# Clustered attention and SwiGLU on one core: routing sims on 16 PE tiles, head group 1 turned by PE, V sums on PE, and a new order on SP and Pool

## The chip, the core and the metric

The kernel runs on one core of one Trainium2 chip. Its engines are named as the profile names them: PE (TensorE, matrix products), PEld (its weight loads), DVE (VectorE), ACT (ScalarE), POOL (GpSimd) and SP, whose queue issues nearly all DMAs. A name with a q, as SPq, is the sequencer of that engine. The metric is the time of one execution in microseconds (us). An execution is counted as slow, and kept out of the ratios, when it is over 1.5% above the fastest of its kernel. One execution of the kernel before, of 369.8 us, is (1.8% above 363.1). A profile is of one execution, and its span is about 1.8 us shorter than the time of the same execution.

## The reference, cut to what matters

```python
# B, H, S, D = 4, 8, 768, 64; 16 clusters; d_model 512, d_ff 1536
q_assign = argmax(q_n @ c_n.T)          # "sims": nearest centroid of each query
k_assign = argmax(k_n @ c_n.T)          # and of each key
mask     = q_assign[:, None] == k_assign[None, :]
attn     = softmax(where(mask, q @ k.T / sqrt(D), -1e9))
x        = (attn @ v)                   # laid out as [B*S, H*D]
out      = (silu(x @ w_gate) * (x @ w_val)) @ w_out
```

## The kernel before

The order on each engine is the order in which the program emits its operations. The emission is driven by *units*. A unit is two score matmuls, one exponential and six value matmuls; there are 192 (4 batches, 2 halves of the queries, 8 heads, 3 pairs of key blocks). From unit 31 on, FFN matmuls are put between those of the attention. Heads come in 8 groups of four; groups 0 and 1 are batch 0. `put(u, f, ...)` emits `f` after unit `u`.

The sims: 32-row, 32-column products in fp32, each in its own tile of the PE array, first for two of the four row groups (8 tiles), then for the other two. Each half uses one of the two score slots (tag `sc`), except for group 1.

```python
def route_sims(qi, bp):                       # bp = 0, 1: half of the rows
    ...
    for t in range(2):
        for s in range(2):
            for bb in range(2):
                p0 = 32 * (2 * bp + bb)
                for i in range(4):
                    nc.tensor.matmul(
                        out=sps[bb][32 * i:32 * i + 32, 0:SH // 2],
                        lhsT=c4[p0:p0 + 32, 4 * g + i, s, t, :],
                        rhs=qts[(qi, i)][p0:p0 + 32, t, :, s, :], ...)
    ...
    nc.vector.transpose(out=dst, in_=sp[:, :, 0:SH // 2])
```

Only group 0 is turned to [D, tokens] by PE; all others by DMA transposes, each of which waits at the head of the SP queue for Pool's cast:

```python
if qi == 0:   # 12 PE transposes into PSUM, two ScalarE copies
    ...
else:
    nc.sync.dma_start_transpose(out=qka..., in_=nb...)
```

The V sums of groups 2 to 7 are a VectorE reduction and one fp32 matmul with ones. The attention output `xn` of a head pair becomes a column block of `xall` by a DMA transpose, emitted at once. Weights are loaded in 18 pieces into 4 staging buffers and cast by Pool.

The softmax here doesn't subtract the row's maximum and nothing guards it: scores larger than these inputs give would overflow.

## Time and profile before

The median is 365.0 us (363.1 to 369.8). Unit 0 starts at 18.2 us, the first FFN matmul is at 52.8. The table of windows of the kernel before (for each stretch: length, then busy us and count of PE, PEld, DVE, ACT, POOL, then the granted PE clock, DMA share, GB/s; the DMA share is the summed time of the packets over that of 16 DMA engines, and can exceed 1):

```profile
18.00:30.00 12.00, 10.66 (x212) 6.80 (x212) 9.79 (x19) 6.51 (x9) 0.96 (x2) 1.00 1.06 161
30.00:42.00 12.00, 9.84 (x87) 6.01 (x86) 8.71 (x13) 6.97 (x10) 6.01 (x6) 0.72 1.12 301
42.00:52.00 10.00, 8.71 (x107) 4.19 (x103) 3.45 (x6) 9.21 (x13) 6.80 (x7) 1.00 1.10 347
52.00:66.00 14.00, 9.75 (x86) 5.76 (x85) 6.64 (x12) 8.07 (x13) 5.39 (x6) 1.00 1.10 320
66.00:90.00 24.00, 21.63 (x293) 13.70 (x293) 20.06 (x35) 12.34 (x19) 12.44 (x18) 1.00 1.03 227
90.00:120.00 30.00, 26.23 (x308) 15.55 (x312) 18.86 (x31) 14.62 (x23) 5.32 (x8) 0.94 0.72 180
120.00:320.00 200.00, 198.56 (x2173) 123.36 (x2183) 126.37 (x228) 134.68 (x201) 34.59 (x49) 1.00 0.42 100
```

From 120 us on PE is hardly idle (busy 198.56 of 200 us), so there only PE work counts. Before that it is, and the DMA engines are full from 18 to 90 us. Between 30 and 42 us the clock was at one half for part of the time (33.6 to 40.5 in the clock records). What PE waited for, longest first (us in total, times, longest):

```profile
PE vp L395 <- DVE ug L415: 4.2, 3, 1.7
PE sc L336 <- DMA qka<-ohT: 2.6, 2, 2.3
PE gp L395 <- DMA xall<-xn: 2.0, 1, 2.0
PE sc L336 <- DVE qka L214: 1.9, 2, 1.6
PE acc L362 <- ACT pt_118 L343: 1.3, 5, 0.4
PE gp L395 <- DVE hT L425: 1.3, 1, 1.3
```

From the timeline of the same kernel (start, length, engine, line, operation, out<-in, then the idle time before it and what ended it). The SP queue spends 18.1 to 26.6 us on four DMA transposes of group 1. Only then comes the first weight load, and Pool, which casts it, sat idle for 10 us. ScalarE lost 3.75 us to the sims of group 1:

```profile
18.14 1.36 SPq L244 DMA_TRANSPOSE qka<-nb_93  x1
...
24.60 1.98 SPq L244 DMA_TRANSPOSE qka<-nb_96  x1
...
26.62 1.40 SPq L202 DMA_DIRECT2D wt<-in_moe_w_gate_dram  x1
...
27.90 0.81 ACT L343 ACTIVATE pt_120<-sc 128x768 bf16<-128x768 f32 x1 [3.75 <-PE sc L336]
...
32.43 1.17 POOL L206 CAST wg_sb<-wt 128x1024 bf16<-128x1024 f32 x1 [10.15 <-DMA wt<-in_moe_w_gate_dram]
```

The sims of a later group, in the stretch where PE is full. Each half takes 1.46 us from its first start to the next matmul:

```profile
163.76 1.53 PE L269 MATMUL sp<-qt,c_68 32*32 32x192 f32 x64
...
165.22 0.50 PE L336 MATMUL sc<-qka 80*128 80x384 bf16 x2
...
167.14 1.53 PE L269 MATMUL sp<-qt,c_68 32*32 32x192 f32 x64
...
168.60 0.50 PE L336 MATMUL sc<-qka 80*128 80x384 bf16 x2
```

### The profile page before, as it was taken

What the parts mean: (1) busy time and instruction counts of PE and PEld (TensorE: products, weight loads), DVE (VectorE), ACT (ScalarE), POOL (GpSimd) and SP (SyncE); (2) the same over time, 40 slices, a digit from 0 to 9 for tenths busy, and PEclk for the clock granted to TensorE, in tenths of its full rate; (3) what the DMA queues carried; (4) which work ended last, traced back from release to release, by engine and by line L of the source; (5) the groups of instructions that cost most, each with busy time, mean ns of one, the idle gap of its engine ahead of it and who ended that gap; (6) DMA issues with size and microseconds to landing.
All of it is one profiled execution on the core that took longest, in us unless ns stands there. A gap on an engine that the chain in (4) does not pass through costs nothing.

```text
span 363.9 us, 9129 instructions
## 1 busy us (share of the span) xinstructions
PE 341.2 (94%) x3751; PEld 210.6 (58%) x3770; DVE 226.6 (62%) x403; ACT 220.0 (60%) x328; POOL 82.9 (23%) x118
## 2 busy tenths in 40 slices
PE   8987978896898899999999999999999999999995
PEld 6854535563465565666556665666566656665652
DVE  7779425779249966586828784777636614660770
ACT  5546785454356546674667656765677777774431
POOL 5513564715203300141003300420100100000000
PEclk9998799999899999999999999999999999999999
DMA  7699999999687532895267513962220011002102
GB/s 239 244 189 268 287 278 365 259 186 263 132 252 174 84 73 58 265 211 56 60 201 205 112 24 84 324 140 34 61 70 11 14 42 68 13 13 70 40 0 86
DMA packets 82712, 50.55 MB, mean 139 GB/s; under 512 B 59248, under 2 KB 77680, under 8 KB 82672
## 3 DMA queue, kind: packets, MB, share of 16 engines
q1 hardware_dynamic: 82528, 49.95, 54.6%
q8 instruction: 29, 0.48, 0.6%
q14 instruction: 11, 0.09, 0.1%
q10 hardware_dynamic: 144, 0.03, 0.0%
HBM read 28.34 MB, written 6.29 MB: 95 GB/s over the span
## 4 chain that ended last, share of the span: by engine, by line
PE 68%; DMA 14%; DVE 6%; SPq 6%; POOL 3%; issue 2%; ACT 1%; DVEq 0%; POOLq 0%; ACTq 0%
PE o_ps L437 16%; PE gp L395 13%; PE vp L395 13%; PE sc L336 12%; PE acc L362 7%; DMA wt<-in_moe_w_gate_dram 5%; PE sp L269 4%; SPq L244 4%; DMA qk<-in_k_dram 4%; PE gv L395 2%; DMA vs<-in_v_dram 2%; DMA qka<-ohT 2%; DMA wt<-in_moe_w_out_dram 2%; DVE qt L223 2%; DVE ug L415 1%
## 5 line engine op out<-in xcount | busy, mean ns | idle before, releaser
L336 PE MATMUL sc<-qka 80*128 80x384 bf16 x384 | 96.1, 332 | 4.5 <-DMA qka<-ohT 2.6
L415 DVE SCALAR_TENSOR_TENSOR ug<-th,gp 128x384 f32<-128x384 f32 x90 | 49.2, 547 | 52.2 <-ACT th L413 51.9
L395 PE MATMUL vp<-xall,wv_sb 128*128 128x384 bf16 x360 | 73.2, 325 | 4.5 <-DVE ug L415 4.2
L395 PE MATMUL gp<-xall,wg_sb 128*128 128x384 bf16 x360 | 73.4, 325 | 3.2 <-DMA xall<-xn 2.0
L381 POOL TENSOR_TENSOR xn<-num,rec 128x384 bf16<-128x384 f32 x28 | 23.1, 826 | 211.2 <-DVE rec L379 143.2
L437 PE MATMUL o_ps<-wo_sb,hT 128*128 128x512 bf16 x269 | 70.1, 384 | 1.0
L343 ACT ACTIVATE pt_118<-sc 128x768 bf16<-128x768 f32 x48 | 39.0, 812 | 38.7 <-PE sc L336 38.1
L425 DVE TENSOR_TENSOR hT<-ug,vp 128x384 bf16<-128x384 f32 x90 | 49.4, 549 | 10.2 <-PE vp L395 3.2
L413 ACT ACTIVATE th<-gp 128x384 f32<-128x384 f32 x90 | 43.9, 488 | 18.7 <-PE gp L395 15.8
L395 PEld LDWEIGHTS <-wv_sb 128*128 128x128 bf16 x384 | 37.2, 97 | 30.8 <-issue 5.9
L395 PEld LDWEIGHTS <-wg_sb 128*128 128x128 bf16 x384 | 37.2, 97 | 29.5 <-issue 3.9
L343 ACT ACTIVATE pt_121<-sc 128x768 bf16<-128x768 f32 x48 | 38.9, 811 | 20.6 <-PE sc L336 20.6
L343 ACT ACTIVATE pt_119<-sc 128x768 bf16<-128x768 f32 x48 | 38.9, 811 | 17.9 <-PE sc L336 17.5
L343 ACT ACTIVATE pt_120<-sc 128x768 bf16<-128x768 f32 x48 | 39.0, 812 | 17.7 <-PE sc L336 15.8
L437 PEld LDWEIGHTS <-hT 128*128 128x128 bf16 x288 | 28.1, 98 | 29.4 <-issue 2.0
L223 DVE STREAM_TRANSPOSE qt<-qk 128x768 f32<-128x768 f32 x32 | 30.7, 963 | 7.4 <-DMA qk<-in_k_dram 7.3
L336 PEld LDWEIGHTS <-qka 80*128 80x128 bf16 x384 | 25.4, 99 | 10.2 <-issue 6.3
L269 PE MATMUL sp<-qt,c_68 32*32 32x192 f32 x1024 | 24.6, 324 | 0.2 <-DVE sT L280 0.2
L442 ACT ACTIVATE o_sb<-o_ps 128x512 f32<-128x512 f32 x24 | 14.4, 598 | 12.1 <-PE o_ps L437 12.1
L362 PEld LDWEIGHTS <-pt_118 128*128 128x128 bf16 x288 | 14.8, 98 | 11.7 <-ACT pt_118 L343 4.2
L362 PEld LDWEIGHTS <-pt_120 128*128 128x128 bf16 x288 | 15.0, 98 | 11.1 <-ACT pt_120 L343 3.2
L374 DVE TENSOR_TENSOR num<-acc,vsb_109 128x390 f32<-128x390 f32 x12 | 6.7, 561 | 22.0 <-PE acc L362 22.0
(115 smaller groups left out, 349.7 us busy)
## 6 DMA issues: line engine op xcount, KB each, us to landing
vs<-in_v_dram SPq DMA_DIRECT2D x16, 384.0 KB, 5.4
out_dram<-o_sb SPq DMA_DIRECT2D x24, 256.0 KB, 2.2
qk<-in_q_dram SPq DMA_DIRECT2D x14, 384.0 KB, 5.2
qk<-in_k_dram SPq DMA_DIRECT2D x14, 384.0 KB, 5.7
wt<-in_moe_w_gate_dram SPq DMA_DIRECT2D x6, 512.0 KB, 6.0
wt<-in_moe_w_val_dram SPq DMA_DIRECT2D x6, 512.0 KB, 6.1
wt<-in_moe_w_out_dram SPq DMA_DIRECT2D x6, 512.0 KB, 7.3
qka<-ohT SPq DMA_DIRECT2D x24, 48.0 KB, 2.1
```

Of the source, the lines that this page charges most:

```text
L223: nc.vector.transpose(out=qt.rearrange("p t j s i -> p (t j s i)"), in_=qk.rearrange("p t j d -> p (t j d)"))
L244: nc.sync.dma_start_transpose(out=qka.rearrange("p t j n -> p (t j) n"), in_=nb.rearrange("p t j c -> p (t j c)"))
L269: nc.tensor.matmul(out=sps[bb][32 * i:32 * i + 32, 0:SH // 2], lhsT=c4[p0:p0 + 32, 4 * g + i, s, t, :], rhs=qts[(qi, i)][p0:p0 + 32, t, :, ...
L336: nc.tensor.matmul(out=sc[:, jj, 0:SH], lhsT=qka[0:KA, 1, j, :], rhs=qka[0:KA, 0, JH * hf:JH * hf + JH, :], start=True, stop=True)
L343: nc.scalar.activation(out=pt, in_=sc[:, :, 0:SH], func=ACT.Exp, scale=SCALE)
L362: nc.tensor.matmul(out=acc[:, h % 2, a, :], lhsT=pt[:, jj, ts(a, 128)], rhs=va[:, h % 4, j, :], start=(h % 2 == 0 and j == 0 and a == 0), ...
L381: (nc.vector if xc == 0 and qi < NQ else nc.gpsimd).tensor_tensor(out=xn.rearrange("p a h d -> p h a d"), in0=num[:, :, :, 0:D], in1=rec.t ...
L395: nc.tensor.matmul(out=ps, lhsT=w[:, c, ts(fb, 128)], rhs=xall[:, ch % XR, c, :], start=(c == 0), stop=(c == DMC - 1))
L413: nc.scalar.activation(out=th, in_=gp, func=ACT.Tanh, scale=0.5)
L415: nc.vector.scalar_tensor_tensor(out=ug, in0=th, scalar=1.0, in1=gp, op0=ALU.add, op1=ALU.mult)
L425: nc.vector.tensor_tensor(out=hTs[ch][:, fb, :], in0=ug, in1=vp, op=ALU.mult)
L437: nc.tensor.matmul(out=ops[0], lhsT=hT[:, fc, ts(ob, 128)], rhs=wo_sb[:, fc, :], start=(fc == 0), stop=(fc == DFC - 1))
```

## The change

The intent: run the sims of a group in one burst on all 16 tiles, holding both score slots at once, with FFN matmuls issued before the next scores; turn group 1 by PE and ScalarE like group 0, so that the SP queue and the DMA engines are free for weights; move V sums from VectorE to PE; and reorder loads. Weight casts were on Pool already; what moves to Pool are group 0's V casts. The diff, cut to its core:

```diff
-    W1 = 40                 # warming matmuls (they only keep PE busy) before unit 0
+    W1 = 8                  # now put twice, so 16
+    XD = 4                  # units by which three of the first four x transposes are put off
     def sum_v(qi):                            # groups 2 to 7, as group 0 and 1 before
-        nc.vector.tensor_reduce(out=vs1, in_=vaugs[qi % NV]..., op=ALU.add)
-        ... one fp32 matmul with ones_f
+        for j in range(J):
+            nc.tensor.matmul(out=vp, lhsT=ones_b, rhs=vaugs[qi % NV][:, :, j, :], ...)
     def cast_v(qi, i):
-        copy(nc.scalar if qi == 0 else nc.gpsimd, ...)
+        copy(nc.gpsimd, ...)
     def prep_cast(qi, i):
-        if qi == 0:
+        if qi < NQ:                           # group 1 too: PE transposes, ScalarE copies
     def route_sims(qi, rows=4, tag="sc", part=0):
-                for bb in range(2):
-                    p0 = 32 * (2 * bp + bb)
+                    for bb in range(rows):
+                        p0 = 32 * (b0 + bb)
     def normalise(...):
+        if xc or qi >= NQ:
+            turn_x(xc, m)
+        else:
+            put(cur[0] + (XD if m < 3 else 0), turn_x, xc, m)
-    wu = [3, 5, 6, 8, 9, ..., 31]; the last five loads (14th to 18th) not before unit 26
+    wu = [2, 3, 5, 6, 8, 9, ..., 30]; each load one unit after the cast that frees its buffer
-            w0 = (30, 42)[n] if b == 1 else ...
+            w0 = (28, 42)[n] if b == 1 else ...
-            for bp in range(2):
-                put(w0 + 8 + bp, route_sims, qi, bp)
+            put(w0 + 8, route_sims, qi)
+            early.add(w0 + 9)                 # scores of this unit after its FFN matmuls
-            warm(W2)
+            warm(3 if ui < 8 else W2)
... (group 1's sims in two units; its mask copies in units 7, 14 and 15, not all in 6;
...  group 0's V sum one unit earlier; `xn` of batch 0's second half on VectorE, not Pool)
```

More of the change, by code (lines that the diff above doesn't have):

```diff
@@ L120 @@
            for i in range(NV)]
-    ones_f = persist.tile([128, 128], FP32, name="ones_f")
-    nc.gpsimd.memset(ones_f, 1.0)
     ones_b = persist.tile([128, 128], BF16, name="ones_b")
@@ L140, in cast_v, with sum_v @@
     def cast_v(qi, i):
-        copy(nc.scalar if qi == 0 else nc.gpsimd,
-             vaugs[qi % NV][:, i, :, 0:D], vst.pop((qi, i)))
-    def sum_v0(qi):
+        copy(nc.gpsimd, vaugs[qi % NV][:, i, :, 0:D], vst.pop((qi, i)))
+    def sum_v(qi):
         vp = psum.tile([128, 4, D + 1], FP32, name="vsq", tag="f", bufs=3)
         for j in range(J):
-            nc.tensor.matmul(out=vp, lhsT=ones_b, rhs=vaugs[qi][:, :, j, :],
+            nc.tensor.matmul(out=vp, lhsT=ones_b,
+                             rhs=vaugs[qi % NV][:, :, j, :],
                              start=(j == 0), stop=(j == J - 1))
-        nc.vector.tensor_scalar_mul(vsb[qi], vp, TINY)
-    vs1s = {}
-    def sum_v(qi):
-        vs1 = sb.tile([128, 4, D + 1], FP32, name="vs1", tag="num", bufs=2)
-        nc.vector.tensor_reduce(
-            out=vs1, in_=vaugs[qi % NV].rearrange("p i j c -> p i c j"),
-            axis=AX.X, op=ALU.add)
-        vs1s[qi] = vs1
-    def sum_vm(qi):
-        vs1 = vs1s.pop(qi)
-        vp = psum.tile([128, 4 * (D + 1)], FP32, name="vsp", tag="f", bufs=3)
-        nc.tensor.matmul(out=vp, lhsT=ones_f,
-                         rhs=vs1.rearrange("p i c -> p (i c)"),
-                         start=True, stop=True)
-        nc.vector.tensor_scalar_mul(
-            vsb[qi % NV].rearrange("p i c -> p (i c)"), vp, TINY)
+        nc.vector.tensor_scalar_mul(vsb[qi % NV], vp, TINY)
     NP = 4
@@ L221, in prep_turn @@
         qk = qk_tiles[(b, 4 * g + i)]
-        qt = sb.tile([128, 2, J, 2, 32], FP32, name="qt", tag="qt", bufs=4)
+        spare = qi == 1 and i == 0
+        qt = sb.tile([128, 2, J, 2, 32], FP32, name="qt",
+                     tag="hT" if spare else "qt", bufs=1 if spare else 4)
         nc.vector.transpose(out=qt.rearrange("p t j s i -> p (t j s i)"),
@@ L251, with route_sims @@
     rmaxs = {}
-    def route_sims(qi, bp):
+    def route_sims(qi, rows=4, tag="sc", part=0):
         b, g = quads[qi]
-        if bp == 0:
+        if part == 0:
             routes[qi] = sb.tile([128, 2, 2 * J, 2, NCL], FP32, name="sT",
                                  tag="sT", bufs=2)
-        if qi == 1:
-            sps = [psum.tile([128, 512], FP32, name="sp", tag="f", bufs=3)
-                   for _ in range(2)]
-        else:
-            sp = psum.tile([128, 2, 512], FP32, name="sp", tag="sc", bufs=2)
-            sps = [sp[:, bb] for bb in range(2)]
-        for t in range(2):
-            for s in range(2):
-                for bb in range(2):
-                    p0 = 32 * (2 * bp + bb)
-                    for i in range(4):
-                        nc.tensor.matmul(
-                            out=sps[bb][32 * i:32 * i + 32, 0:SH // 2],
-                            lhsT=c4[p0:p0 + 32, 4 * g + i, s, t, :],
-                            rhs=qts[(qi, i)][p0:p0 + 32, t, :, s, :],
-                            start=(t == 0 and s == 0),
-                            stop=(t == 1 and s == 1),
-                            skip_group_check=True)
-        dst = routes[qi][:, bp].rearrange("p m t c -> p (m t c)").rearrange(
-            "p (b n) -> p b n", b=2)
-        if qi == 1:
-            for bb in range(2):
-                nc.vector.transpose(out=dst[:, bb],
-                                    in_=sps[bb][:, 0:SH // 2])
-        else:
-            nc.vector.transpose(out=dst, in_=sp[:, :, 0:SH // 2])
@@ new lines, in route_sims @@
+        for b0 in (rows * part,):
+            if tag == "sc":
+                sps = [psum.tile([128, 2, 512], FP32, name="sp", tag="sc",
+                                 bufs=2) for _ in range(rows // 2)]
+                ps = [sps[bb // 2][:, bb % 2] for bb in range(rows)]
+            else:
+                sps = [psum.tile([128, 1, 512], FP32, name="sp", tag="f",
+                                 bufs=3) for _ in range(rows)]
+                ps = [sps[bb][:, 0] for bb in range(rows)]
+            for t in range(2):
+                for s in range(2):
+                    for bb in range(rows):
+                        p0 = 32 * (b0 + bb)
+                        for i in range(4):
+                            nc.tensor.matmul(
+                                out=ps[bb][32 * i:32 * i + 32, 0:SH // 2],
+                                lhsT=c4[p0:p0 + 32, 4 * g + i, s, t, :],
+                                rhs=qts[(qi, i)][p0:p0 + 32, t, :, s, :],
+                                start=(t == 0 and s == 0),
+                                stop=(t == 1 and s == 1),
+                                skip_group_check=True)
+            n = rows // len(sps)
+            for m, sp in enumerate(sps):
+                c0 = (b0 + n * m) * J
+                nc.vector.transpose(
+                    out=routes[qi].rearrange("p a m t c -> p (a m) t c")[
+                        :, c0:c0 + n * J].rearrange(
+                            "p m t c -> p (m t c)").rearrange(
+                                "p (b n) -> p b n", b=n),
+                    in_=sp[:, :, 0:SH // 2])
@@ L380, in normalise, with turn_x @@
         xn = sb.tile([128, JH, 2, D], BF16, name="xn", tag="xn", bufs=2)
-        (nc.vector if xc == 0 and qi < NQ else nc.gpsimd).tensor_tensor(
+        (nc.vector if qi < NQ else nc.gpsimd).tensor_tensor(
             out=xn.rearrange("p a h d -> p h a d"), in0=num[:, :, :, 0:D],
             in1=rec.to_broadcast([128, 2, JH, D]), op=ALU.mult)
+        xns[(xc, m)] = xn
+        if xc or qi >= NQ:
+            turn_x(xc, m)
+        else:
+            put(cur[0] + (XD if m < 3 else 0), turn_x, xc, m)
+    xns = {}
+    cur = [0]
+    def turn_x(xc, m):
         nc.sync.dma_start_transpose(
             out=xall[:, xc, m, :].rearrange("p (a t) -> p a t", a=JH),
-            in_=xn.rearrange("p a h d -> p (a h d)"))
+            in_=xns.pop((xc, m)).rearrange("p a h d -> p (a h d)"))
     hTs = {}
@@ L501 @@
     centroids_T(1)
-    for i in range(2, 4):
-        prep_turn(0, i)
+    prep_turn(0, 2)
     prep_cast(0, 2)
+    prep_turn(0, 3)
+    prep_turn(1, 0)
+    route_sims(0)
+    prep_cast(0, 3)
     for bp in range(2):
-        route_sims(0, bp)
         route_max(0, bp)
-    prep_cast(0, 3)
     route_hot(0)
@@ L511 @@
         route_back(0, t)
-    warm(W1)
+    for i in range(2):
+        prep_cast(1, i)
+        warm(W1)
     for i in range(4):
@@ L515 @@
     load_v(1, 1)
-    for i in range(4):
-        prep_cast(1, i)
     for i in range(2):
@@ L523 @@
     put(0, load_w, 3)
-    put(0, prep_turn, 1, 0)
-    put(0, prep_turn, 1, 1)
-    put(0, prep_mask, 0, 2, nc.vector)
-    put(0, prep_turn, 1, 2)
-    put(0, prep_turn, 1, 3)
-    put(0, prep_mask, 0, 3, nc.vector)
-    put(3, sum_v0, 0)
+    for i in range(1, 4):
+        put(0, prep_turn, 1, i)
+    for i in range(2, 4):
+        put(0, prep_mask, 0, i, nc.vector)
+        put(i, prep_cast, 1, i)
+        put(1, cast_v, 1, i - 2)
+        put(1, cast_v, 1, i)
+    put(2, sum_v, 0)
     for bp in range(2):
-        put(S1, route_sims, 1, bp)
-        put(S1, route_max, 1, bp)
-    put(S1, route_hot, 1)
+        put(S1 + bp, route_sims, 1, 2, "f", bp)
+        put(S1 + bp, route_max, 1, bp)
+    put(S1 + 1, route_hot, 1)
     for t in range(2):
-        put(S1, route_back, 1, t)
+        put(S1 + 1, route_back, 1, t)
     for i in range(4):
-        put(S1 + 1, prep_mask, 1, i, nc.vector)
-        put(1, cast_v, 1, i)
-    put(13, sum_v0, 1)
-    wu = [3, 5, 6, 8, 9, 10, 12, 13, 15, 16, 18, 19, 26, 27, 28, 29, 30, 31]
+        put(S1 + 2 + (0, 0, 7, 8)[i], prep_mask, 1, i, nc.vector)
+    put(13, sum_v, 1)
+    wu = [2, 3, 5, 6, 8, 9, 10, 12, 13, 15, 16, 18, 19, 26, 27, 28, 29, 30]
     for i in range(len(wjobs)):
@@ L544 @@
         if i + 4 < len(wjobs):
-            put(wu[i] + 1 if i < 9 else max(wu[i] + 1, 26), load_w, i + 4)
+            put(wu[i] + 1, load_w, i + 4)
+    early = set()
     for b in range(1, B):
@@ L549 @@
             qi = NQ * b + n
-            w0 = (30, 42)[n] if b == 1 else u0 + (P0, P1)[n]
+            w0 = (28, 42)[n] if b == 1 else u0 + (P0, P1)[n]
             for m in range(2):
@@ L558 @@
                 put(w0 + 14 + i, prep_mask, qi, i, nc.sync)
-            put(w0 + 15, sum_v, qi)
-            put(w0 + 19, sum_vm, qi)
+            put(w0 + 16, sum_v, qi)
+            put(w0 + 8, route_sims, qi)
+            early.add(w0 + 9)
             for bp in range(2):
-                put(w0 + 8 + bp, route_sims, qi, bp)
                 put(w0 + 9 + bp, route_max, qi, bp)
@@ L570 @@
     for ui, u in enumerate(units):
-        pt = att_scores(u)
+        cur[0] = ui
+        if ui not in early:
+            pt = att_scores(u)
         if ui < 24:
-            warm(W2)
+            warm(3 if ui < 8 else W2)
         want = per * min(
@@ L581 @@
             fpos += 1
+        if ui in early:
+            pt = att_scores(u)
         if pend is not None:
```

## The prediction

> **What bounds the kernel now.** Three stages, by the table of windows.
> 1. 18 to 52.7 us, attention alone (units 0 to 30; unit 31 brings the first FFN matmul, at 52.7). An exponential takes 0.81 us, so 31 units need 25 us; they take 34.5. Lost: ScalarE idles 3.7 us behind the sims of head group 1 (timeline), PE waits 1.6 us for that group's mask copies, then the granted clock is one half from 33.6 to 40.5, which the Trainium skill ("TensorE: Matmul & The Clock Gate", Part 1) puts down to an idle window. Four DMA transposes of group 1 hold the SP queue from 18.1 to 26.6, so the first weight load is issued only at 26.6; the DMA share is above 1.0 until 66, and the chain of waits runs through weight, v and qk loads to 64.9.
> 2. 52.7 to 120: PE starves. From starts of matmuls against their streaming time I find 18.4 us of gaps, 4 of them sims. Named PE waits: x transpose 2.0, values behind VectorE 4.2 (which itself waits 6.8 for qk loads and holds a 2.82 us V reduction per group), mask DMA 2.6; half clock at 92.
> 3. 120 to 364: PE full (198.6 of 200 us), so only PE work counts.
>
> **Costs.**
> - Sims: 64 matmuls on 8 tiles take 1.46 us: eight starts 6.7 ns apart, one batch per 163 ns, so the tiles bound it. 16 tiles could stream 128 in 1.4 us, but weight loads sometimes come 16.7 ns apart; I estimate 1.7 to 2.0 in place of 2.93, and 0.3 for one tile mode change less. (Same page, Part 3: a further tile costs about 4 ns.) 1.2 us for each of 6 groups on the full PE: -7. Both score slots are taken, so scores wait for two 0.58 us turns on VectorE; FFN matmuls issued first hide most: +1.
> - V sums: six 260-column bf16 matmuls, 0.72 us, for two fp32 ones, 0.52: +1.2; VectorE loses 2.82 per group.
> - Group 1 by PE: 48 transposes, eight 0.72 us copies on ScalarE, half in units 2 and 3: +2.9 of ScalarE there; weights start near 16.5 us.
> - Unit 0 starts as now (18.2 to 18.6).
>
> **On the critical path.** First FFN matmul: 18.5 + units 0 to 8 about 12.5 + 23 x 0.82 + 1 of stalls, near 50.5: -2. Stage 2: of 12.5 us of removable gaps 8.5 go (qk loads and masks earlier, no V reduction). With sims -7, V sums +1.2, slot waits +1: -15.5, over half from stage 2.
>
> **Predicted: 350 us**, 343 to 357. Faster by over 2%: 0.90; within 2%: 0.09; slower: 0.01.
>
> **What the profile would show.** First weight load issued at 15 to 18 us; first FFN matmul at 49 to 52; no half clock between 30 and 42; sims x128 in 1.7 to 2.0 us; PE waits from there to 120 below 5 us, none on mask DMA, x transposes near zero; from the first FFN matmul to the end about 298 us, not 311; VectorE 15 us less busy.
>
> **What would make it wrong.** Sims bound by issue (2.5 us or more): +5. Scores stalled by the slots over 0.5 us per group. Pool is in order: group 1's last casts stand behind V and weight loads, so PE could wait in unit 3 and lose the clock (16 warming matmuls, not 40): +3. Stage 2's gaps are DMA bandwidth and stay: +6. All gaps go: 342.

## The result, and the profile after

The changed kernel takes 353.2 us (352.4 to 354.5, four runs); before, in the same rounds, 365.0 (364.5 without the slow execution). The ratio is 0.9697 with a 95% interval of 0.9639 to 0.9755. Ratios are the mean time of one kernel's fast runs over that of the other's fast runs of the same rounds, so not quite the ratio of the medians. The profiled span fell from 363.9 to 352.7 us, by 11.2.

The windows of the kernel after, in the same columns and stretches as before:

```profile
18.00:30.00 12.00, 10.63 (x204) 8.11 (x210) 5.94 (x11) 8.29 (x11) 9.24 (x11) 1.00 0.97 298
30.00:42.00 12.00, 9.66 (x143) 5.77 (x126) 11.26 (x19) 7.89 (x11) 6.30 (x7) 1.00 1.06 324
42.00:52.00 10.00, 8.74 (x108) 4.30 (x109) 3.47 (x6) 9.24 (x13) 4.68 (x5) 1.00 1.10 272
52.00:66.00 14.00, 11.68 (x96) 6.86 (x94) 9.18 (x15) 8.08 (x13) 7.37 (x10) 0.88 0.99 239
66.00:90.00 24.00, 22.41 (x305) 13.95 (x304) 18.96 (x35) 13.14 (x21) 5.75 (x8) 1.00 0.62 163
90.00:120.00 30.00, 29.51 (x424) 18.66 (x429) 21.64 (x41) 18.23 (x29) 6.55 (x10) 1.00 0.84 189
120.00:320.00 200.00, 199.70 (x2206) 123.66 (x2179) 112.34 (x220) 136.74 (x205) 32.22 (x45) 1.00 0.39 97
```

PE is now full from 90 us on, the DMA share is below 1 from 52 us on instead of 90, and DVE has 14 us less in the last stretch. What PE waits for after:

```profile
PE gp L392 <- DMA xall<-xn: 2.3, 1, 2.3
PE sc L323 <- DVE qka L195: 1.8, 2, 1.3
PE vp L392 <- DVE ug L412: 1.3, 2, 0.8
...
PE tp L221 <- POOL nb_95 L215: 1.0, 2, 0.8
```

The mask DMA (2.6 us) is gone from the list and the wait behind VectorE fell from 4.2 to 1.3. The x transpose is still there and is now the longest.

Because the chain of the first 60 us shifts from one limit to another, the most useful comparison is by units, at places where both programs have done the same work. Starts of score matmuls, read from the two traces:

| stretch | before, us | after, us | difference |
|---|---|---|---|
| start to unit 0 | 18.2 | 17.6 | -0.6 |
| unit 0 to unit 32 (attention, first FFN block) | 37.7 | 39.0 | +1.4 |
| unit 32 to unit 62 (FFN beside attention, sims of groups 2 and 3) | 66.8 | 58.3 | -8.6 |
| unit 62 to the end (PE full, sims of groups 4 to 7) | 241.2 | 237.8 | -3.4 |

The whole gain comes after unit 32. The first stage, where I had expected 2 us, gave nothing: units 0 to 8 took 13.9 us (10.8 before), units 8 to 31 took 21.2 (23.6 before, 6.8 of them at half clock). The timeline of the kernel after shows two waits in it; the experiments below test both. The first weight load is indeed issued 10.7 us earlier. But Pool, in order, casts group 1's V first and waits 1.89 us for its load; `nb_95` and `nb_96`, the inputs of PE's transposes in units 2 and 3, stand behind that and behind a weight cast:

```profile
15.89 0.47 SPq L183 DMA_DIRECT2D wt<-in_moe_w_gate_dram  x1
...
18.75 1.42 POOL L195 CAST vaug_106<-vs 128x384 bf16<-128x384 f32 x3 [1.89 <-DMA vs<-in_v_dram]
...
20.11 0.83 POOL L215 CAST nb_95<-qk 128x768 bf16<-128x768 f32 x1
...
20.99 0.86 PE L221 MATMUL tp<-ident_b,nb_95 128*64 128x128 bf16 x12 [0.80 <-POOL nb_95 L215]
21.51 1.37 POOL L187 CAST wg_sb<-wt 128x1024 bf16<-128x1024 f32 x1 [0.57 <-DMA wt<-in_moe_w_gate_dram]
...
22.83 0.82 POOL L215 CAST nb_96<-qk 128x768 bf16<-128x768 f32 x1
...
23.71 0.86 PE L221 MATMUL tp<-ident_b,nb_96 128*64 128x128 bf16 x12 [0.22 <-POOL nb_96 L215]
```

And at the end of the stage, the last x transpose of the first half batch is issued at 49.41 behind the loads of group 2. It lands at 55.97, 6.6 us later, where all x transposes of this kernel have a median of 2.4. The first FFN block gets three of its four matmuls done and stops:

```profile
47.16 0.47 SPq L87 DMA_DIRECT2D qk<-in_q_dram  x1
...
47.68 0.47 SPq L87 DMA_DIRECT2D qk<-in_k_dram  x1
...
49.41 1.19 SPq L381 DMA_TRANSPOSE xall<-xn  x1
...
53.06 0.65 PE L392 MATMUL gp<-xall,wg_sb 128*128 128x384 bf16 x3
...
56.01 0.48 PE L392 MATMUL gp<-xall,wg_sb 128*128 128x384 bf16 x1 [2.30 <-DMA xall<-xn]
```

The clock records then show one half from 55.8 to 59.2 us. In the kernel before, the last two of these transposes landed at 55.3 and 55.5 and PE waited 2.0 us for them: the DMA queue set the start of the FFN in both. The other profiles agree: in ten of the eleven that make this transpose by DMA, unit 32 starts 0.4 to 0.7 us after it lands (landings from 54.8 to 61.0 us). The exception is u_sched, where it starts 1.9 us after.

The sims after, in the stretch where PE is full. One burst takes 2.26 us to the next matmul, and FFN matmuls follow without a gap while VectorE turns the two slots:

```profile
154.90 2.33 PE L255 MATMUL sp<-qt,c_68 32*32 32x192 f32 x128
...
157.14 1.05 DVE L265 STREAM_TRANSPOSE sT<-sp 128x384 f32<-128x384 f32 x2 [1.08 <-PE sp L255]
...
157.17 0.82 PE L392 MATMUL gp<-xall,wg_sb 128*128 128x384 bf16 x4
...
157.83 0.81 PE L392 MATMUL vp<-xall,wv_sb 128*128 128x384 bf16 x4
...
158.48 0.49 PE L323 MATMUL sc<-qka 80*128 80x384 bf16 x2
```

With the 0.12 us between the matmul before and the burst, a group costs 2.26 + 0.12 = 2.38 us in place of 2 x (1.46 + 0.12) = 3.17 (from unrounded starts): 0.79 us less.

### The profile page after: what moved, and what is told of

It reads as the page before. It is cut to its first block, busy times and chain, and to the rows that moved or that the text cites. A ratio compares the mean times of both kernels' runs of the same rounds, so it can differ in the third digit from the quotient of the medians.

```text
span 352.7 us, 9271 instructions
## 1 busy us (share of the span) xinstructions
PE 335.5 (95%) x3834; PEld 206.9 (59%) x3834; DVE 211.1 (60%) x401; ACT 222.9 (63%) x332; POOL 82.6 (23%) x117
## 4 chain that ended last, share of the span: by engine, by line
PE 79%; DVE 9%; DMA 4%; ACT 3%; issue 2%; POOL 2%; SPq 0%; ACTq 0%; DVEq 0%; POOLq 0%
PE o_ps L434 18%; PE gp L392 15%; PE vp L392 15%; PE sc L323 14%; PE acc L349 9%; PE sp L255 4%; PE gv L392 2%; DMA xall<-xn 2%; DMA vs<-in_v_dram 2%; PE vsq L145 1%; DVE ohT L299 1%; DVE ug L412 1%; DVE hT L422 1%; ACT pt_116 L330 1%; DVE num L361 1%
## 5 line engine op out<-in xcount | busy, mean ns | idle before, releaser
L323 PE MATMUL sc<-qka 80*128 80x384 bf16 x384 | 94.5, 327 | 1.8 <-DVE qka L195 1.8
L412 DVE SCALAR_TENSOR_TENSOR ug<-th,gp 128x384 f32<-128x384 f32 x90 | 49.3, 548 | 65.7 <-ACT th L410 65.2
L434 PE MATMUL o_ps<-wo_sb,hT 128*128 128x512 bf16 x288 | 71.5, 378 | 0.0
L368 POOL TENSOR_TENSOR xn<-num,rec 128x384 bf16<-128x384 f32 x24 | 19.8, 827 | 198.6 <-DVE rec L366 137.1
L330 ACT ACTIVATE pt_117<-sc 128x768 bf16<-128x768 f32 x48 | 38.9, 811 | 12.9 <-PE sc L323 12.5
L349 PEld LDWEIGHTS <-pt_118 128*128 128x128 bf16 x288 | 15.0, 98 | 13.0 <-issue 4.4
L349 PEld LDWEIGHTS <-pt_116 128*128 128x128 bf16 x288 | 14.7, 97 | 10.5 <-ACT pt_116 L330 3.6
L255 PE MATMUL sp<-qt,c_68 32*32 32x192 f32 x1024 | 19.8, 330 | 0.2 <-DVE qt L206 0.2
L349 PEld LDWEIGHTS <-pt_119 128*128 128x128 bf16 x288 | 14.9, 97 | 8.5 <-ACT pt_119 L330 1.7
```

The lines of the kernel that those rows point to most:

```text
L255: nc.tensor.matmul(out=ps[bb][32 * i:32 * i + 32, 0:SH // 2], lhsT=c4[p0:p0 + 32, 4 * g + i, s, t, :], rhs=qts[(qi, i)][p0:p0 + 32, t, :, ...
L323: nc.tensor.matmul(out=sc[:, jj, 0:SH], lhsT=qka[0:KA, 1, j, :], rhs=qka[0:KA, 0, JH * hf:JH * hf + JH, :], start=True, stop=True)
L330: nc.scalar.activation(out=pt, in_=sc[:, :, 0:SH], func=ACT.Exp, scale=SCALE)
L349: nc.tensor.matmul(out=acc[:, h % 2, a, :], lhsT=pt[:, jj, ts(a, 128)], rhs=va[:, h % 4, j, :], start=(h % 2 == 0 and j == 0 and a == 0), ...
L368: (nc.vector if qi < NQ else nc.gpsimd).tensor_tensor(out=xn.rearrange("p a h d -> p h a d"), in0=num[:, :, :, 0:D], in1=rec.to_broadcast( ...
L412: nc.vector.scalar_tensor_tensor(out=ug, in0=th, scalar=1.0, in1=gp, op0=ALU.add, op1=ALU.mult)
```

## The experiments

Twelve runs were made, in three calls, each with its own runs of the kernel before. The third call (after_again, b_sims16, x4_pe, x4_lag) was on another chip than the first two, so compare ratios, not medians, across calls. The column "to unit 32" and the next two are read from each run's trace, as in the table above.

| run | median us | ratio to before | to unit 32 | unit 32 to 62 | unit 62 to end |
|---|---|---|---|---|---|
| before | 365.0 | 1 | 55.8 | 66.8 | 241.2 |
| changed kernel | 353.2 | 0.9697 | 56.6 | 58.3 | 237.8 |
| after_again (the same) | 353.7 | 0.9741 | 56.6 | 56.4 | 237.8 |
| u_sims8 | 360.3 | 0.9863 | 60.1 | 60.1 | 240.9 |
| u_pe1 | 360.9 | 0.9908 | 61.7 | 58.3 | 238.4 |
| u_vsum | 356.1 | 0.9784 | 57.9 | 60.9 | 238.1 |
| u_sched | 357.4 | 0.9810 | 59.1 | 61.5 | 238.0 |
| u_xd | 358.4 | 0.9849 | 60.0 | 58.3 | 237.8 |
| pool_order | 354.8 | 0.9732 | 58.4 | 59.1 | 237.8 |
| x3_pe | 350.9 | 0.9644 | 54.3 | 56.4 | 238.1 |
| x4_pe | 351.9 | 0.9661 | 56.5 | 57.2 | 238.7 |
| x4_lag | 354.0 | 0.9722 | 59.0 | 54.1 | 238.8 |
| b_sims16 (from before) | 359.5 | 0.9867 | 55.5 | 63.4 | 238.2 |
| halfcols | 387.0 | 1.0613 | 58.0 | 68.4 | 257.9 |

Intervals of these ratios are about 0.003 to 0.007 to each side, so differences below some 2 us in the medians are not decided; the last column repeats within a few tenths in all runs with the same sims, and carries more.

### How much one run differs from the next: after_again

The edit: none.

> The changed kernel again, for the spread of its first stage from run to run. Theory: the same program has two ways through the first stage, with and without a half clock near 24 us after PE has waited for the V load's casts on Pool; times 352 to 356, the profiled first FFN matmul at 53 or near 56. Rival: it repeats within 0.3 per cent.

Times were 352.6 to 357.5 us. The profiled execution had its first FFN matmul at 55.5 instead of 53.1, because PE waited 3.4 us for mask copies and had the half clock from 38.7 to 42.1. It had no half clock near 24, so that part of my guess did not show, and the spread was over 0.3 per cent. What is instructive: the x transpose landed at 56.2 (55.97 in the first profile), so this execution lost its time earlier and then did not wait for x, and unit 32 started at 56.6 in both. In this pair of profiles the time lost in the attention units, up to the landing of x, cost nothing; that landing was the limit of the stage.

### Sims undone: u_sims8

```diff
-            put(w0 + 8, route_sims, qi)
-            early.add(w0 + 9)
             for bp in range(2):
+                put(w0 + 8 + bp, route_sims, qi, 2, "sc", bp)
```

> The changed kernel with only the sims of groups 2 to 7 put back to 8 tiles in two halves. Theory: the sims gain is the PE time of the bursts, 2.26+0.12 us against 2x(1.46+0.12), so 0.79 us for each of 6 groups: this run is 4.7 us slower than the changed kernel (profiled span near 357.4). Rival: the two score slots held at once cost some of it, so undoing costs less, 2 us or below. Second rival, my prediction: 6 to 7 us.

In the last stretch, with four groups, it took 240.9 us in place of 237.8: 3.1 us, or 0.77 for each group, which is the 0.79 read from the bursts. So the slots cost nothing there. The total is 1.7% above the changed kernel (0.9863 to 0.9697), which is more than 6 x 0.79 = 4.7 us; 3.5 us of the profiled difference lie before unit 32, where the two programs emit the same work, and so probably belong to the spread of the first stage. The intervals of the two ratios leave some 3 to 9 us for the total, so it does not contradict 4.7. The theory stands, by the stretches and not by the total.

### Sims alone, on the kernel before: b_sims16

The edit puts the changed kernel's 16-tile burst and its `early` rule for groups 2 to 7 into the kernel before, and nothing else.

> The kernel before with one part of the change alone: the sims of groups 2 to 7 on 16 tiles over both score slots. Theory: a burst of 128 takes 2.01 us between its first and last start and 0.25 to the next matmul, as in the changed kernel, in place of 2 x 1.46 and two more gaps of 0.12; 4 to 4.7 us faster than before, scores never waiting for a slot. Rival: what the changed kernel gained from them depended on its other parts; under 2 us.

It took 0.9867 of before, 4.8 us less. The last stretch went from 241.2 to 238.2 us, 0.77 for each group again. This part is worth the same with and without the others.

### What bounds a burst: halfcols

Simplified:

```diff
+for hc in range(2):                      # groups 2 to 7
     nc.tensor.matmul(
-        out=ps[bb][32 * i:32 * i + 32, 0:SH // 2], ...
+        out=ps[bb][32 * i:32 * i + 32, 96 * hc:96 * hc + 96], ...
-        rhs=qts[(qi, i)][p0:p0 + 32, t, :, s, :],
+        rhs=qts[(qi, i)][p0:p0 + 32, t, 3 * hc:3 * hc + 3, s, :],
```

> The changed kernel with each sims matmul of groups 2 to 7 cut into two of 96 columns: the same results, the same columns streamed, twice the instructions. Theory: a 16-tile burst is bound by the supply of weight load and matmul pairs, 2.0 us / 128 = 15.7 ns a pair; then 256 pairs take near 4.0 us, span about +12 us. Rival: the tiles or the result banks bound it; then the burst stays at 2.0 to 2.3 us and the span within 2 us.

The result was wrong (relative error 0.79). The Trainium skill, "PSUM — Partial Sum Buffer" (Terms, "Zero region"), states that a matmul that starts an accumulation clears the written bits of the whole bank for its quadrants; the second half's start then makes the first half's next product overwrite instead of add. The wrong result is consistent with this; no run tests it alone. No instruction of the kernel depends on the values, so the times still tell. A burst of 256 took 4.4 to 6.3 us between its first and last start in the four that ran at full clock (two more, 6.6 and 7.4, ran in part at half clock), for the same number of columns, and in places PE waited for nothing that the profile shows:

```profile
172.10 2.73 PE L258 MATMUL sp<-qt,c 32*32 32x96 f32 x154
...
175.46 1.81 PE L258 MATMUL sp<-qt,c 32*32 32x96 f32 x102 [0.63 <-issue]
```

So columns streamed do not bound a 16-tile burst. That the number of weight load and matmul pairs does is likely; the starts in the burst of the changed kernel point the same way:

```
ns from the first start, before (64 on 8 tiles), 163.8 us:   0 6 13 20 26 33 40 46 | 186 193 ... 233 | 349 356 ... 396 | 511 ...
ns from the first start, after (128 on 16 tiles), 154.9 us:  0 7 13 20 27 33 40 47 | 135 142 ... | 543 559 576 593 609 626 643 659 ...
```

On 8 tiles, eight starts 6.7 ns apart and then a pause to the next batch 163 ns on. On 16 tiles most starts are about 16.7 ns apart (75 of the 127 steps are 15 to 19 ns); at that pace each tile has its turn once in 16 x 16.7 = 267 ns, less often than the 163 ns that it allowed on 8 tiles, so there the tiles are not the limit. Why this edit cost more than twice is not settled: it also put two matmuls in a row on the same tile.

### Group 1 back on DMA transposes: u_pe1

```diff
-        if qi < NQ:
+        if qi == 0:
```

> The changed kernel with head group 1 turned by DMA transposes again instead of PE and ScalarE. Theory: turning by PE buys nothing in the first stage (its 3 us of ScalarE copies and the waits for them cost what the freed SP queue gives), but it takes four DMA transposes off a full DMA; so here the first FFN matmul comes 1.5 to 3 us earlier, near 51, the first weight load near 19 to 22, and the x transpose and group 2's loads land later, so that gaps from the first FFN matmul to 120 us grow by 3 us or more: the run 1 to 4 us slower than the changed kernel. Rival: the move did not pay; faster by 1 to 3 us.

The first FFN matmul came at 52.2, only 0.9 us earlier, although PE had the half clock from 17.4 to 24.3. But the last x transposes landed at 61.0 instead of 56.0, and PE's longest wait became

```profile
PE gp L392 <- DMA xall<-xn: 8.5, 3, 5.0
```

Half clock followed from 55.0 to 65.2. The run is 2.2% above the changed kernel (0.9908 to 0.9697), more than the 4 us I had allowed, and 5.1 us of it are before unit 32. The four transposes keep SP until 29.4 us, the loads behind them shift, and the last x transpose is issued at 54.2 us instead of 49.4. All four executions (359.6 to 362.3 us) lie above all eight of the changed kernel (352.4 to 357.5). So turning group 1 by PE pays by what it takes off the SP and DMA queue; in the attention units themselves this run shows no gain.

### x transposes issued at once: u_xd

```diff
-    XD = 4
+    XD = 0
```

> The changed kernel with the x transposes of the first half batch issued at once (XD 0 instead of 4). Theory: the last one, which PE waits for, is issued at once in both, so under 1 us either way. Rival: SP stands waiting for x while weight loads queue behind it, so the loads and that last transpose land later: 2 us or more slower.

My theory fell. The last transpose was issued at 51.4 instead of 49.4 and landed at 59.3; PE waited 6.0 us for it and ran at half clock from 55.5 to 62.3. The run is 1.6% slower than the changed kernel (0.9849 to 0.9697), and its four times (357.9 to 361.2 us) lie above all eight of the changed kernel, if by little. In the profile all of it is before unit 32 (60.0 to 56.6); the later columns are the same to 0.1 us. The first of these transposes, emitted before its input is ready, waits at the head of SP: from 26.2 to 31.4 us SP issues nothing, where the changed kernel issued three weight loads. The loads so held come to stand in front of the transpose that matters.

### V sums back on VectorE: u_vsum

The edit restores the reduction and the fp32 matmul for groups 2 to 7.

> The changed kernel with the V sums of groups 2 to 7 back on VectorE (2.82 us reduction and an fp32 matmul of 0.52 us instead of six bf16 ones, 0.69 us). Theory: after 120 us PE is full, so that part is 4 x 0.17 = 0.7 us faster; between the first FFN matmul and 120 us VectorE's queue holds up PE by 1 to 2 us for two groups; net within 1.5 us of the changed kernel. Rival: the gain of the second stage comes mainly from these reductions; then 3 us or more slower.

Ratio 0.9784, 0.9% above the changed kernel (0.4% above its repetition; the intervals overlap). Unit 32 to 62 took 60.9 us in place of 58.3 and 56.4 in the two profiles of the changed kernel. In the last stretch, where PE is full and the edit takes 4 x 0.17 = 0.7 us of work off it, it was 0.3 us slower, not faster. The direction of the theory for the second stage held, but its gain after 120 us did not appear.

### Weight and group 2 schedule as before: u_sched

The edit restores `wu`, the rule that held later loads until unit 26, and `w0 = 30` for group 2.

> The changed kernel with the weight casts and loads at their old units (loads after the ninth not before unit 26) and group 2's preparation two units later, as before. Theory: these two are what took the mask wait (2.3 us) and the half clock at 92 us away; both come back and VectorE waits longer for qk loads: 3 to 5 us slower than the changed kernel. Rival: under 1 us.

Ratio 0.9810, 1.2% above the changed kernel, inside the expected 3 to 5 us, though the intervals overlap (0.9742 to 0.9879). The half clock near 90 came back (88.0 to 91.4), and PE waited 4.0 us behind VectorE; the mask wait itself did not come back. Its attention stage was also long (unit 31 at 57.9, half clock twice), so that x had landed before the FFN began; how much of that is the edit and how much the spread is open.

### Pool's casts moved ahead: pool_order

```diff
     for i in range(4):
         cast_v(0, i)
     load_v(1, 1)
+    for i in range(2, 4):
+        cast_nb(1, i)                     # the Pool half of prep_cast(1, i)
```

> The changed kernel with the two Pool casts of head group 1's heads 2 and 3 issued before the V casts and the weight cast; PE's transposes stay where they were. Theory: the first stage did not get shorter because PE waits in units 2 and 3 for these casts, which stand behind a V load and a weight load on Pool; then units 3 and 4 come 1.5 to 2.5 us earlier, the first FFN matmul at 51 to 51.7 us instead of 53.1, span 1 to 2 us less. Rival: ScalarE's added copies and the later mask chain set the stage; then the first FFN matmul stays within 0.5 us of 53.1.

The theory fell; the rival's outcome held, its mechanism was not tested: the first FFN matmul came at 52.8, within 0.3 us. PE did not wait for Pool in units 2 and 3 any more, but unit 4 started at 24.6 us all the same (24.5 before the edit), now after a wait of 0.69 us for VectorE at the transposes. And x landed at 57.7, so unit 32 was later, not earlier.

### The x transpose that PE waits for, by PE: x3_pe

```diff
-            put(cur[0] + (XD if m < 3 else 0), turn_x, xc, m)
+            put(cur[0] + (XD if m < 3 else 2), turn_x, xc, m)
...
+        if xc == 0 and m == 3 and cur[0] < NU + 4:
+            for a in range(JH):
+                nc.tensor.transpose(out=tp[:, a, :], in_=xn[:, a, :], identity=ident_b)
+            nc.vector.tensor_copy(out=xall[:, xc, m, :]..., in_=tp[:, 0:JH, :])
+            return
```

> The changed kernel with one x transpose, the last of the first half batch, made by PE (3 transposes) instead of a DMA transpose. Theory: that DMA transpose, issued at 49.4 and landed at 56.0 us behind the loads of group 2, is what PE waits 2.3 us for, and the idle PE loses the clock from 55.8 to 59.2; without it both go, span 3 to 4 us less. Rival: the FFN start waits for something else next (VectorE behind qk loads), so less than 1 us.

The profiled span fell to 348.8 us, 3.9 below the first profile of the changed kernel and 2.0 below the repeated one. No wait for x is left among PE's waits (the longest are below), there is no half clock before 347 us, and unit 32 starts at 54.3 instead of 56.6:

```profile
PE acc L349 <- ACT pt L330: 2.0, 7, 0.5
PE wp L475 <- DVE wz L101: 1.1, 1, 1.1
PE tp L221 <- POOL nb L215: 1.0, 2, 0.8
```

The edit was three PE transposes and a VectorE copy in place of one DMA transpose, emitted two units later. The median is 350.9 us, ratio 0.9644 (0.9589 to 0.9700): the lowest and clearly below before. Against the changed kernel the intervals overlap (0.9639 to 0.9755, and 0.9676 to 0.9806 on repetition), so about 0.5 to 1% better is likely and not proven.

### All four by PE, and the FFN earlier: x4_pe and x4_lag

x4_pe makes all four x transposes of the first half batch by PE and includes the edit of pool_order; x4_lag adds `LAG0 = 4` (FFN from unit 28) and `S1 = 4`.

> The changed kernel with all four x transposes of the first half batch on PE, two units after their values, and the two Pool casts moved ahead. Theory: SP never stands waiting for x during the weight loads and PE never waits for a transpose behind the loads; first FFN matmul at 52 to 53, no wait on x there, no half clock at 56: 348 to 351 us, 1 per cent below the changed kernel. Rival: the twelve extra PE transposes and four VectorE copies lengthen the first stage by as much as they save.

> The run above with the FFN started three units earlier (unit 28) and group 1's sims one unit earlier. Theory: ScalarE bounds the first stage and leaves PE about 0.3 us idle per unit, so FFN matmuls put there fill it: 1 to 2 us faster than the run above. Rival: VectorE stands at unit 28 waiting for group 2's qk load and holds the FFN up; no gain or slower.

x4_pe: 351.9 us, ratio 0.9661, 0.4 to 0.8% below the two ratios of the changed kernel, so not clearly better, and no better than one transpose by PE. There was no wait on x and no half clock at 56, as expected, but unit 0 came only at 20.4 us: the half clock lay from 7.1 to 10.5 in that execution. x4_lag: 354.0 us, not faster than x4_pe (0.9722 to 0.9661, the intervals overlap). It gained 3.2 us from unit 32 to 62, since more of the FFN was done by then, and lost 2.4 before unit 32; among its waits is 3.0 us of PE for `xn` of VectorE at the new transposes. So the rival's outcome is what the numbers show, though it named another wait of VectorE.

## Why the prediction was right or wrong

The predicted time was 350, range 343 to 357; measured 353.2, faster by over 2%. So the outcome was as predicted; the span fell by 11.2 us where I had expected 15.5. In part this was luck: two gains stayed out or came smaller (first stage, sims) and two small costs did not appear (slot waits, V sums), which offset part of it.

- **"First FFN matmul ... near 50.5: -2": wrong.** It came at 53.1 and 55.5 in two profiles, against 52.8. Units 0 to 8 took 13.9 us, not 12.5: PE stood 1.0 us behind Pool's casts, as the last paragraph of the prediction had warned. But with these moved ahead (pool_order) units 0 to 8 still took 13.3 us; what sets this length is open. Units 8 to 31 took 21.2, not 23 x 0.82 = 18.9: among others a mask wait of 1.35 us. But the deeper error is that the step looked at the wrong end. Unit 32 starts when the last x transpose has landed, 56.0 against 55.5 before: after_again lost time in the attention units without a later unit 32, u_xd landed it later and unit 32 with it.
- **"x transposes near zero": wrong.** 2.3 us, and a half clock after it. With this one DMA transpose taken away (x3_pe) the span is 3.9 us below the first profile's and 2.0 below the repeated one's; the span was 4.3 us above the expected one.
- **Sims "-7", slot waits "+1": the direction was right, both sizes off.** I estimated 1.7 to 2.0 us for a burst and compared it with 2 x 1.46, which includes the way out to the next matmul; on the same footing the burst is 2.26. Measured, 0.79 for each group from the starts, 0.77 by both experiments, so -4.7 for six. Slot waits were nil within 0.1 us a group, since the two figures agree. Starts 16.7 ns apart, which the prediction took for occasional, fill most of the burst.
- **V sums "+1.2": right on PE** (six matmuls take 0.69 us for 0.52, 1.0 in all), but u_vsum shows that in the last stretch this loss does not appear in the time. That VectorE's freedom pays for it there is likely; no run shows it alone.
- **Stage 2, "of 12.5 us of removable gaps 8.5 go": about right in size.** Unit 32 to 62 is 8.6 us shorter, 10.4 in the repeated profile; two groups' sims, counted apart in the prediction, are 1.6 of this, so 7.0 and 8.8 stand against the 8.5. By u_vsum the V sums are worth 2.6 to 4.5 us there and by u_sched the schedule 3.2 to 5.1; the two overlap, and no run undoes both. Waits of PE there are below 5 us and the mask DMA is not among them, as predicted.
- **Other signs.** First weight load at 15.9 us (15 to 18 predicted); from the first FFN matmul to the end 299.6 (298 predicted, 311 before); VectorE 226.6 to 211.1 us busy, 15.5 less (15 predicted). "No half clock between 30 and 42" held in the first profile and not in the repeated one.

What stays open: the spread of the first 56 us, up to 5 us between executions of nearly the same program, is not explained: the half clock falls in other places from one execution to the next, but u_pe1 had it for 6.8 us (17.4 to 24.3) and still reached unit 31 sooner than the changed kernel. So costs that lie before unit 32 in one profile (u_sims8, part of u_sched; the size of u_pe1's and u_xd's, though not their sign) cannot be told from it. Two parts of the change were not undone: the warming matmuls, and `xn` of batch 0's second half on VectorE.

## What to carry to other kernels

When a stage is limited by the landing of one transfer, as unit 32 was here, shortening other work before it gives nothing: find the landing, and ask what stands before it in its queue. A small transfer with a deadline should not be queued behind large ones; three PE transposes in place of one DMA transpose were worth 2 to 4 us of the profiled span, as much as some of the larger edits, though the ratios do not yet prove it. Compare two schedules at points where both have done the same work, because the sum of the waits moves from place to place from one execution to the next.

## What the Trainium skill lacked or had wrong

- "TensorE: Matmul & The Clock Gate", Part 3 (Measured speedup vs the span model), gives about 4 ns for each further tile. Here the first starts are 6.7 ns apart, and in a burst of 128 fp32 pairs on 16 tiles most are about 16.7 ns apart, 2.01 us in all. The page has no sustained rate for tiles that each need a weight load.
- The same page, Part 1, has a floor of about 25 ns from start to start of matmuls however small. On 32 x 32 tiles it does not hold: 6.7 ns. Part 3 of the page implies as much, but the sentence makes no exception.
- The same page, Part 1, puts the half clock down to an idle window of about 3.4 us. Here a single PE wait of 2.3 us (53.7 to 56.0) was followed by it, for 3.4 us (55.8 to 59.2), and a wait of 6.0 us in u_xd by it for 6.8; without the wait (x3_pe) it did not come. So here an idle stretch shorter than a whole window was enough. Further on, Part 1 lets short idle stretches do it too, but gives no length.
- "TensorEngine Tiling (Array Packing)", Key Properties, says "Mode switching requires drain" and gives no cost. Around each burst of sims the trace shows 0.12 us from the last start before it and 0.25 us from its last start to the next matmul; how much of this is the switch, no run shows.
- No page that I used tells how long a DMA transpose takes to land in a full queue: 6.6 us for the one that mattered, 2.4 as the median of all 32 of its kind.
